# Writing the attention exponentials to PSUM and normalising from there, in a fused attention and feed-forward kernel on one core

## The chip, the core and the metric

The kernel runs on one core of one Trainium2 chip. The core has five engines that take their instructions in order and meet only at semaphores: TensorE (PE in the profile, its weight loads PEld), VectorE (DVE), ScalarE (ACT), GpSimd (POOL) and SyncE (SP, which issues DMAs here). TensorE writes its results to PSUM, a memory of 8 banks that VectorE and ScalarE can read and write; everything else lies in SBUF. The metric is the device time of the whole program in microseconds (us), the median of three runs.

## The reference

The program is a local attention (4 batches, 8 heads, 576 positions, head size 64, a window of the last 64 positions) followed by two feed-forward parts without a residual. Cut to what matters:

```python
scores = (q @ k.T) / sqrt(64)
scores = where(0 <= i - j < 64, scores, -1e9)
scores = scores - scores.max(-1)
attn   = exp(scores)
attn   = attn / (attn.sum(-1) + 1e-09)
x      = attn @ v                        # (2304, 512)
x      = ((x @ w1) * (x @ w2)) @ w3 @ w_out
h      = x @ w_in                        # (2304, 2048)
return (h * sigmoid(h)) @ w_out2
```

The weights arrive as float64 and are turned into float32, or into a high and a low part, on the chip.

## The kernel before

**Attention.** The 2304 tokens are cut into 18 units of 128, the 8 heads into 4 pairs, so there are 72 groups g, of one unit and one pair each. For a group, `scores(g)` multiplies queries with 192 keys for each of two heads into one PSUM tile `s` (128 x 2 x 192 float32, one bank, one buffer); two VectorE instructions on line 344 add the mask, scale and store the negated scores in the SBUF tile `sm` and their minimum in `nm`. `exps(g)` runs two ScalarE instructions (line 355, one for each head) that replace `sm` by its exponential in place and sum it into a small tile `es`. `normalise(g)` is three VectorE instructions: a sum of `es` (363), a reciprocal (365) and a product over `sm` in place (367). `transposes(g)` (377) has TensorE transpose `sm` in three pieces into the PSUM tile `t` (one bank, one buffer); `split_t(g)` copies it out on ScalarE (383, or 387 and 389) and, for later groups, takes the rounding remainder on VectorE (390, 392). `values(g)` multiplies with v into `o`.

**Two kinds of groups.** `plain(g)` is true for the first 17 groups (0 to 16), whose products run in float32. The other 55 use high and low parts.

**What sets the order.** The order on each engine is the order in which the code is written. `half(h)` does half a group: the even half of group g issues `scores(g)`, `values(g-2)`, `transposes(g-1)` with their copies, then `exps(g)`; the odd half issues `normalise(g)`, the sum of the values of g-2 (`total`: lines 419 and 420 on ScalarE, 421 and 422 on VectorE, 423 on GpSimd), and the preparation of the next queries and keys (297 on ScalarE, 309 on VectorE, 303 on GpSimd). `halves_to` puts one half before each unit of the dense work. In the first part (`phase_w`, up to about 91 us) that work is the conversion of the weights and the product of w3 and w_out (`accw`). In blocks 0 to 5 of 384 tokens (`phase_a`) a unit is 12 TensorE products of 128x384: first 16 units of x @ w1 and x @ w2 (`ab`, line 618; ScalarE copies one result, line 632, and VectorE multiplies the other into it, line 634, after which ScalarE casts it, line 85), then 8 units of the product with w3 @ w_out (`x`, line 648, copied out on line 601). `split_x` rounds the attention's result for the next block (lines 85 and 88, out of tile `xr`). The attention of the last group ends at about 403 us; what follows is the second feed-forward part, TensorE work without attention.

**Banks.** `s`, `t`, `o` and the conversion's `z` have one PSUM bank each, the accumulators of the dense work four.

Of the kernel before, what the change touches and what calls it, by code (L numbers as in the profile page):

```python
# [9 lines left out]
F32 = mybir.dt.float32  # L10
# [3 lines left out]
AF = mybir.ActivationFunctionType  # L14
ALU = mybir.AluOpType
# [19 lines left out]
def mask_kind(u):  # L35
    at = (u * 128) % S
    if at == 0:
        return 1
    return 2 if at + 128 > S else 0
# [3 lines left out]
def tile_window_attention_ffn(ctx, tc, qkv, qkp, vp, mask, w1, w2, w3t, w_out, w_in, w_out2, out):  # L43
# [7 lines left out]
    nc = tc.nc  # L51
# [5 lines left out]
    psa = late.enter_context(tc.tile_pool(name="psa", bufs=1, space=PSUM))  # L57
# [155 lines left out]
    def fill(n=1):  # L213

        for _ in range(min(n, len(parts))):
            parts.pop(0)()
# [18 lines left out]
    def drain():  # L235
# [7 lines left out]
    qk_raw, v_raw, qk_st, v_st, s_st, p_st = {}, {}, {}, {}, {}, {}  # L243
# [6 lines left out]
    sums_of = [  # L250
        att.tile([128, 16], F32, name=f"es{i}", tag=f"es{i}", bufs=1)[:, 0:4].rearrange("p (h n) -> p h n", h=2)
        for i in range(2)
    ]
# [7 lines left out]
    def plain(g):  # L261


        return g < PLAIN

    def place(g):
        blk, r = divmod(g, 3 * NPAIR)
        return blk * 3 + r % 3, r // 3
# [55 lines left out]
    def scores(g):  # L324
        s_ps = psa.tile([128, 2, 192], F32, name=f"s{g}", tag="s")
        t = qk_raw.pop(g) if plain(g) else qk_st.pop(g)
        if plain(g):
            k = t.rearrange("p (h n) -> p h n", h=2)[:, :, 0:192]
            nc.tensor.matmul(s_ps, lhsT=t[:, 192:320], rhs=k, start=True, stop=True)
        else:  # L330
            for h in range(2):

                nc.tensor.matmul(  # L333
                    s_ps[:, h], lhsT=t[:, 128 + h * 128 : 256 + h * 128],
                    rhs=t[:, 384 + h * 192 : 576 + h * 192], start=(h == 0), stop=False,
                )
            nc.tensor.matmul(s_ps, lhsT=t[:, 0:128], rhs=k_lo[g % 2], start=False, stop=True)
        nm = att.tile([128, 2], F32, name=f"nm{g}", tag="nm", bufs=2)
        rs = att.tile([128, 2], F32, name=f"rs{g}", tag="rs", bufs=2)
        fill(2)  # L340
        at = mask_at[mask_kind(place(g)[0])]
        for h in range(2):

            nc.vector.tensor_tensor_reduce(  # L344
                out=sm[g % 2][:, h, :], in0=s_ps[:, h, :], in1=consts[:, at + 64 - 64 * h : at + 256 - 64 * h],
                op0=ALU.add, op1=ALU.min, scale=-(D ** -0.5), scalar=3.0e38, accum_out=nm[:, h : h + 1],
            )
        fill()
        s_st[g] = (nm, rs)

    def exps(g):
        nm, rs = s_st[g]
        for h in range(2):
            x = sm[g % 2][:, h, :]
            nc.scalar.activation(  # L355
                out=x, in_=x, func=AF.Exp, scale=-1.0, bias=nm[:, h : h + 1], accum_out=sums_of[g % 2][:, h, 0:1]
            )

    def normalise(g):
        _, rs = s_st.pop(g)  # L360
        x = sm[g % 2]
        fill()
        nc.vector.tensor_reduce(out=rs, in_=sums_of[g % 2], axis=mybir.AxisListType.X, op=ALU.add)
        fill()
        nc.vector.reciprocal(out=rs, in_=rs)
        fill()
        nc.vector.tensor_tensor(out=x, in0=x, in1=rs.unsqueeze(2).to_broadcast([128, 2, 192]), op=ALU.mult)

    def transposes(g):

# [56 lines left out]
    def half(h):  # L427
# [4 lines left out]
        if not odd:  # L432
            if g < NG:
                scores(g)
# [7 lines left out]
            if g < NG:  # L442
                exps(g)
        else:
            if g < NG:
                normalise(g)
# [36 lines left out]
    def phase_w():  # L483
# [63 lines left out]
        for f in line[1].stage1():  # L547
            f()
        scores(0)
        spin(1)  # L550
        line[2].stage0(0)
        exps(0)
        line[2].stage0(1)
        for f in line[2].stage1():
# [118 lines left out]
    with tc.manual_schedule():  # L673
# [58 lines left out]
        for f in (0, 1, 2, 3, 4, 5, None, None, None, 6, 7, 8, 9, 10, 11, 12, 13, 14, 15):  # L732
# [3 lines left out]
            tag = f"w{f if f < 6 else f + 10 if f < 14 else f - 8}"  # L736
# [404 lines left out]
```

## Time and profile before

| | us |
|---|---|
| median of 3 runs | 841.74 (841.4 to 841.82) |
| the profiled execution, its own time | 841.24 |
| span of that execution in the profile | 839.5 |
| TensorE busy in it | 827.4 (99%) |
| VectorE / ScalarE / GpSimd busy | 615.3 / 561.2 / 529.7 |

The profiled execution's own time is 1.74 us above its span; these lie outside of what the profile shows. A timeline row gives the start in us from the span's beginning, the duration in us, the engine, the line of the kernel, the operation, its output and inputs by the program's names, their shapes and how many instructions the row merges; square brackets tell how long the engine sat idle before it and on what the idle time ended. A busy TensorE is not one at its peak, since a product's recorded time overlaps the next one's. The rows themselves stand below.

### The profile page before, as it was taken

The page shows a single profiled execution, that of the slowest core. Times are in us where ns is not written, and L with a number is a line of the kernel's source. Part 1 is how long each engine was busy: PE and PEld are TensorE (multiplying, and loading weights), DVE is VectorE, ACT ScalarE, POOL GpSimd, SP SyncE. Part 2 cuts the span into 40 slices and gives each one's busy share as a digit, 9 for nine tenths or more (in the row PEclk, how much of TensorE's full clock was granted, in tenths as well). Part 3 has the DMA queues.
Part 4 walks back from the last instruction along what each step waited for, and adds up shares of the span by engine and source line. Part 5 has one row for each costly group of instructions (what it writes and reads, how often), then busy time and mean ns, then how long its engine had stood idle before and what let it go on. Part 6 is the DMA issues. An engine that isn't in the chain of part 4 may idle for free.

```text
span 839.5 us, 14173 instructions
## 1 busy us (share of the span) xinstructions
PE 827.4 (99%) x4418; PEld 745.9 (89%) x4418; DVE 615.3 (73%) x1424; ACT 561.2 (67%) x1390; POOL 529.7 (63%) x588
## 2 busy tenths in 40 slices
PE   7999999999999999999999999999999999999998
PEld 3555799999999999999999988888888888988986
DVE  7889877688888888888368698998644567644544
ACT  6889778898898898898556566556543446443433
POOL 5768666677777677677565577876454456454441
PEclk9999999999999999999999999999999999999999
DMA  9998234444544544543433522301301201201002
GB/s 320 330 321 279 72 107 128 149 127 133 167 150 142 169 156 145 170 157 103 155 134 120 194 76 76 125 26 51 102 26 56 95 26 64 88 25 51 1 1 75
DMA packets 54682, 102.66 MB, mean 122 GB/s; under 512 B 5200, under 2 KB 32592, under 8 KB 54608
## 3 DMA queue, kind: packets, MB, share of 16 engines
q1 hardware_dynamic: 51008, 96.91, 35.5%
q10 hardware_dynamic: 3600, 4.85, 1.6%
q8 instruction: 35, 0.57, 0.3%
q14 instruction: 39, 0.32, 0.1%
HBM read 88.11 MB, written 13.63 MB: 121 GB/s over the span
## 4 chain that ended last, share of the span: by engine, by line
PE 69%; POOL 8%; ACT 6%; issue 4%; DVE 1%; ACTq 0%; POOLq 0%; DVEq 0%
PE o L882 24%; PE ab L618 14%; PE hy L828 12%; PE hx L828 9%; PE x L648 6%; POOL klo L303 2%; POOL vhl L321 1%; ACT sm L355 1%; PE t L377 1%; POOL xr L423 1%; ACT qkhi L297 1%; POOL p L88 1%; POOL cv_b L189 1%; PE o L411 1%; PE s L333 1%
## 5 line engine op out<-in xcount | busy, mean ns | idle before, releaser
L882 PE MATMUL o<-hl,gp 128*128 128x512 f32 x504 | 133.3, 394 | 0.0
L618 PE MATMUL ab<-xa,hl 128*128 128x384 f32 x576 | 119.0, 341 | 0.0
L828 PE MATMUL hy<-xop,j 128*128 128x384 f32 x576 | 115.9, 335 | 0.0
L618 PE MATMUL ab<-xb,hl 128*128 128x384 f32 x570 | 115.2, 334 | 0.0
L88 POOL TENSOR_TENSOR gp<-tmp,gp 128x384 fp32r<-128x384 f32 x56 | 64.1, 1145 | 77.5 <-ACT gp L85 75.9
L828 PEld LDWEIGHTS hy<-xop,j 128*128 128x128 f32 x576 | 102.6, 188 | 9.0 <-DVE tmp L722 1.0
L882 PEld LDWEIGHTS o<-hl,gp 128*128 128x128 f32 x504 | 93.1, 188 | 13.1
L618 PEld LDWEIGHTS ab<-xb,hl 128*128 128x128 f32 x570 | 100.3, 188 | 0.0
L618 PEld LDWEIGHTS ab<-xa,hl 128*128 128x128 f32 x576 | 99.1, 188 | 0.0
L844 ACT ACTIVATE tmp<-hx 128x384 f32<-128x384 f32 x48 | 23.6, 492 | 111.5 <-DVE hx L722 67.8
L722 DVE TENSOR_TENSOR tmp<-hy,tmp 128x384 f32<-128x384 f32 x96 | 53.2, 554 | 56.1 <-PE hy L828 51.5
L828 PE MATMUL hx<-xop,j 128*128 128x384 f32 x432 | 86.6, 335 | 0.0
L882 PE MATMUL o<-hl,gq 128*128 128x512 f32 x324 | 85.9, 393 | 0.0
L88 POOL TENSOR_TENSOR gq<-tmp,gq 128x384 fp32r<-128x384 f32 x36 | 39.0, 1084 | 74.3 <-ACT gq L85 74.3
L828 PEld LDWEIGHTS hx<-xop,j 128*128 128x128 f32 x432 | 76.8, 188 | 4.1
L423 POOL TENSOR_TENSOR xr<-ot 128x128 f32<-128x128 f32 x55 | 32.7, 594 | 73.7 <-DVE ot L422 65.5
L303 POOL TENSOR_TENSOR klo<-qk,qkhi 64x192 fp32r<-64x192 f32 x110 | 67.2, 611 | 7.6 <-ACT qkhi L297 2.7
L882 PEld LDWEIGHTS o<-hl,gq 128*128 128x128 f32 x324 | 60.3, 188 | 11.2
L648 PE MATMUL x<-p,wp 128*128 128x384 f32 x360 | 69.6, 339 | 0.0
L355 ACT ACTIVATE sm<-sm,nm 128x192 f32<-128x192 f32 x144 | 64.5, 450 | 3.9 <-DVE nm L344 2.5
L648 PEld LDWEIGHTS x<-p,wp 128*128 128x128 f32 x360 | 61.9, 188 | 0.0
L145 POOL TENSOR_TENSOR cv_b<-cv_b,cv_r 128x512 int32<-128x512 int32 x32 | 48.6, 1520 | 18.8 <-DVE cv_b L141 9.4
(146 smaller groups left out, 1896.7 us busy)
## 6 DMA issues: line engine op xcount, KB each, us to landing
qk<-in_qkv SPq DMA_DIRECT2D x55, 384.0 KB, 3.1
words<-in_w_out SPq DMA_DIRECT2D x24, 512.0 KB, 5.4
r<-w_in SPq DMA_DIRECT2D x22, 512.0 KB, 3.4
words<-in_w3t SPq DMA_DIRECT2D x16, 512.0 KB, 6.5
words<-in_w SPq DMA_DIRECT2D x16, 512.0 KB, 6.2
xe<-in_w_in SPq DMA_DIRECT2D x16, 512.0 KB, 4.8
v<-in_qkv SPq DMA_DIRECT2D x55, 96.0 KB, 2.7
x2d<-x2s ACTq DMA_DIRECT2D x24, 192.0 KB, 1.9
```

Of the source, the lines that this page charges most:

```text
L88: (nc.vector if eng_lo == "dve" else nc.gpsimd).tensor_tensor(out=lo, in0=src, in1=f32(hi), op=ALU.subtract)
L145: nc.gpsimd.tensor_tensor(out=x, in0=b, in1=self.r, op=ALU.add)
L189: nc.gpsimd.tensor_tensor(out=self.b, in0=self.b, in1=self.r, op=ALU.add)
L303: nc.gpsimd.tensor_tensor(out=k_lo[g % 2][hs, h * 192 : h * 192 + 192], in0=t[hs, n], in1=f32(hi[hs, n]), op=ALU.subtract)
L355: nc.scalar.activation(out=x, in_=x, func=AF.Exp, scale=-1.0, bias=nm[:, h : h + 1], accum_out=sums_of[g % 2][:, h, 0:1])
L423: nc.gpsimd.tensor_tensor(out=xr[:, c, r : r + 128], in0=t[:, 0:128], in1=t[:, 128:256], op=ALU.add)
L618: nc.tensor.matmul(acc, lhsT=w[:, l, fs], rhs=x[k // 2][:, k % 2, r, :], start=(k == 0 and n == 0), stop=(k == 3 and n == 2),)
L648: nc.tensor.matmul(acc, lhsT=wp[f][:, l, o * 128 : (o + 1) * 128], rhs=p[f][:, r, :], start=(f == 0 and n == 0), stop=(f == 7 and n == 2),)
L722: eng.tensor_tensor(out=out, in0=a, in1=b, op=op)
L828: nc.tensor.matmul(bank[name], lhsT=w[:, l, at + kt], rhs=x[:, kt, r, :], start=(fresh and kt == 0 and n == 0), stop=(kt == 1 and n == 2), ...
L844: nc.scalar.activation(out=sg, in_=src, func=AF.Sigmoid)
L882: nc.tensor.matmul(oacc[t], lhsT=g[:, l, cols], rhs=weights["out", 2 * p + i][:, r, :], start=(p == 0 and i == 0 and n == 0), stop=(p == P ...
```

## The change

The exponentials no longer replace `sm` in place. For the 17 plain groups `exps` takes a new tile `e` from the bank of the transposes' tile `t`; for the others it writes over the scores' own tile `s`, which the masked, scaled scores in `sm` have been read from. `normalise` multiplies out of that PSUM tile into `sm`, from which the transposes read as before.

```diff
-        s_st[g] = (nm, rs)
+        s_st[g] = [nm, rs, s_ps]
 
     def exps(g):
-        nm, rs = s_st[g]
+        nm = s_st[g][0]
+        if plain(g):
+            s_st[g][2] = psa.tile([128, 384], F32, name=f"e{g}", tag="t").rearrange("p (h n) -> p h n", h=2)
+        e = s_st[g][2]
         for h in range(2):
             x = sm[g % 2][:, h, :]
             nc.scalar.activation(
-                out=x, in_=x, func=AF.Exp, scale=-1.0, bias=nm[:, h : h + 1], accum_out=sums_of[g % 2][:, h, 0:1]
+                out=e[:, h, :], in_=x, func=AF.Exp, scale=-1.0, bias=nm[:, h : h + 1], accum_out=sums_of[g % 2][:, h, 0:1]
             )
 
     def normalise(g):
-        _, rs = s_st.pop(g)
+        _, rs, e = s_st.pop(g)
...
-        nc.vector.tensor_tensor(out=x, in0=x, in1=rs.unsqueeze(2).to_broadcast([128, 2, 192]), op=ALU.mult)
+        nc.vector.tensor_tensor(out=x, in0=e, in1=rs.unsqueeze(2).to_broadcast([128, 2, 192]), op=ALU.mult)
```

The instructions and their order stay the same on every engine. What changes beside operands is what they wait for. In the lists below a name in brackets is the semaphore of the engine that is waited for; three lines were added, so line 355 is 358 after the change, 377 is 380, 411 and 412 are 414 and 415.

On ScalarE, around the exponentials of group 56 (`nm56`), the program before has:

```order
L387 CAST pt3_957<-t55_4253 128x2x128 [waits PE_49,Activation_49]
L389 CAST pt1_955<-t55_4253 64x64 [waits Activation_49] x2
L355 ACTIVATE sm0_77,es0_86<-sm0_77,nm56_4244 128x192 [waits DVE_49,Activation_49] x2
L632 COPY a3_6_4278<-ab3_12_4265 128x384 [waits PE_49]
L419 COPY ot54_4283<-o54_4249 64x256 [waits Pool_49]
```

and the changed program:

```order
L390 CAST pt3_971<-t55_4270 128x2x128 [waits PE_49]
L392 CAST pt1_969<-t55_4270 64x64 x2
L358 ACTIVATE s56_4257,es0_86<-sm0_77,nm56_4261 128x192 [waits DVE_49,Activation_49]
L358 ACTIVATE s56_4257,es0_86<-sm0_77,nm56_4261 128x192 [waits Activation_49]
L635 COPY a3_6_4295<-ab3_12_4282 128x384 [waits PE_49]
L422 COPY ot54_4300<-o54_4266 64x256 [waits Pool_49]
```

Both write the same PSUM tile now. The count for which the second exponential waits on ScalarE's own semaphore is the one that the first raises when it is done; before, both waited for exponentials of two groups earlier. This holds for all 72 groups. In 16 of the plain groups the first exponential waits in the same way for the copy of line 383 right ahead of it, which reads the bank.

On TensorE, from the scores of group 57 to the transposes of group 56, the program before has:

```order
L333 MATMUL s57_4319<-qkhi57_4212 128x192 [waits DVE_49,PE_49,Activation_49]
L333 MATMUL s57_4319<-qkhi57_4212 128x192
L337 MATMUL s57_4319<-klo1_80,qkhi57_4212 128x384 [waits Pool_49]
L411 MATMUL o55_4329<-pt3_957,vhl55_4214 128x256 [waits DVE_49,Pool_49]
L411 MATMUL o55_4329<-pt3_957,vhl55_4214 128x256
L412 MATMUL o55_4329<-pt1_955,vhl55_4214 128x4x64 [waits DVE_49,Activation_49]
L377 MATMUL t56_4333<-consts_69,sm0_77 128x128 [waits DVE_49,PE_49,Activation_49]
```

and the changed program:

```order
L333 MATMUL s57_4336<-qkhi57_4229 128x192 [waits DVE_49,Activation_49]
L333 MATMUL s57_4336<-qkhi57_4229 128x192
L337 MATMUL s57_4336<-klo1_80,qkhi57_4229 128x384 [waits Pool_49]
L414 MATMUL o55_4346<-pt3_971,vhl55_4231 128x256 [waits Pool_49]
L414 MATMUL o55_4346<-pt3_971,vhl55_4231 128x256
L415 MATMUL o55_4346<-pt1_969,vhl55_4231 128x4x64
L380 MATMUL t56_4350<-consts_69,sm0_77 128x128 [waits PE_49]
```

VectorE's count on which the scores of 57 wait was that of line 344 of group 56; now it is that of the normalisation of group 56, for which the transposes of 56 waited before. The wait has moved from the seventh instruction of the row to the first. In the plain groups it stays with the transposes, since `e` does not lie in the scores' bank.

## Rows read from the trace of the kernel before

**Rows 1.** The page's part 1: busy us, share and instructions by engine.

```profile
PE 827.4 (99%) x4418; PEld 745.9 (89%) x4418; DVE 615.3 (73%) x1424; ACT 561.2 (67%) x1390; POOL 529.7 (63%) x588
```

**Rows 2.** Timeline of ScalarE: the exponentials of group 55.

```profile
313.98 0.46 ACT L355 ACTIVATE sm<-sm,nm 128x192 f32<-128x192 f32 x1
314.34 0.19 ACT L355 ACTIVATION_READ_ACCUMULATOR sm<-sm,nm 128x1 f32 x1
314.44 0.44 ACT L355 ACTIVATE sm<-sm,nm 128x192 f32<-128x192 f32 x1
```

**Rows 3.** Timeline of VectorE: normalising group 55 and what follows.

```profile
315.00 0.16 DVE L363 TENSOR_REDUCE rs<-es 128x2 f32<-128x4 f32 x1 [0.23 <-ACT sm L355]
315.20 0.17 DVE L365 RECIPROCAL rs<-rs 128x2 f32<-128x2 f32 x1
315.40 0.56 DVE L367 TENSOR_TENSOR sm<-sm,rs 128x384 f32<-128x384 f32 x1
...
316.34 0.42 DVE L421 TENSOR_TENSOR ot<-o,ot 64x256 f32<-64x256 f32 x1 [0.38 <-ACT ot L420]
...
317.58 0.56 DVE L634 TENSOR_TENSOR a<-ab,a 128x384 f32<-128x384 f32 x1
318.06 0.35 DVE L344 CUSTOM_DVE_ANT_0 sm<-s,consts 128x192 f32<-128x192 f32 x1
```

**Rows 4.** Timeline of ScalarE: the cast ahead of group 56's copies and exponentials.

```profile
318.17 0.52 ACT L85 CAST q<-a 128x384 fp32r<-128x384 f32 x1 [0.82 <-DVE a L634]
```

**Rows 5.** Timeline of VectorE: the sums (line 363) of groups 26 and 70.

```profile
160.28 0.16 DVE L363 TENSOR_REDUCE rs<-es 128x2 f32<-128x4 f32 x1 [0.22 <-ACT sm L355]
...
394.89 0.16 DVE L363 TENSOR_REDUCE rs<-es 128x2 f32<-128x4 f32 x1 [0.22 <-ACT sm L355]
```

**Rows 6.** Timeline of TensorE: scores of groups 29, 30 and 56, transposes of 55.

```profile
172.67 0.36 PE L333 MATMUL s<-qkhi 128*128 128x192 f32 x2
...
177.91 0.36 PE L333 MATMUL s<-qkhi 128*128 128x192 f32 x2
...
315.31 0.36 PE L333 MATMUL s<-qkhi 128*128 128x192 f32 x2
...
316.10 0.52 PE L377 MATMUL t<-consts,sm 128*128 128x128 f32 x3
```

**Rows 7.** Views of lines 367, 634, 844: count, shortest/median/longest ns, first and last start.

```profile
L367 DVE TENSOR_TENSOR sm<-sm,rs x72: 557/558/1642, 10.7 to 399.2; 128x384 f32<-128x384 f32 x72
...
L634 DVE TENSOR_TENSOR a<-ab,a x48: 546/558/561, 98.5 to 445.5; 128x384 f32<-128x384 f32 x48
...
L844 ACT ACTIVATE tmp<-hx x48: 482/492/494, 452.9 to 823.4; 128x384 f32<-128x384 f32 x48
L844 ACT ACTIVATE tmp<-tmp x48: 522/525/527, 463.6 to 828.3; 128x384 f32<-128x384 f32 x48
```

**Rows 8.** Waits, 140 to 166 us: waiter <- waited for: us in total, times, longest.

```profile
ACT pt L387 <- PE t L377: 2.0, 4, 0.7
```

**Rows 9.** Timeline around the change from block 2 to 3, group 49.

```profile
282.71 1.36 DVE L367 TENSOR_TENSOR sm<-sm,rs 128x384 f32<-128x384 f32 x1
...
285.65 0.52 ACT L85 CAST xb<-xr 128x384 fp32r<-128x384 f32 x1 [1.61 <-POOL xr L423]
```

**Rows 10.** Timeline of the start: groups 11 (77), 14 (93 to 95), 17 and 18 (114).

```profile
77.25 1.35 DVE L367 TENSOR_TENSOR sm<-sm,rs 128x384 f32<-128x384 f32 x1
...
93.12 0.43 ACT L383 COPY pw<-t 128x320 f32<-128x320 f32 x1
93.45 0.46 ACT L355 ACTIVATE sm<-sm,nm 128x192 f32<-128x192 f32 x1
...
95.02 1.56 DVE L367 TENSOR_TENSOR sm<-sm,rs 128x384 f32<-128x384 f32 x1
...
114.49 0.56 DVE L367 TENSOR_TENSOR sm<-sm,rs 128x384 f32<-128x384 f32 x1
...
114.67 0.36 PE L333 MATMUL s<-qkhi 128*128 128x192 f32 x2
```

## The prediction, made before the changed kernel was run

> **What bounds the kernel now.** I read the busy times first: TensorE is busy 99% of the span [rows 1], so the end moves only if TensorE waits longer or less. The change leaves its instructions and their order alone, so I looked for its waits: on the timeline, group by group, and from there at what releases them.
>
> After block 0, attention is a ring between ScalarE and VectorE. In group 55 the two exponentials start at 313.98 and 314.44 [rows 2]; behind them ScalarE has the copies of lines 632, 419 and 420, and these end the idle time of VectorE ahead of line 421 at 316.34, and VectorE's row goes on to line 634, which ends at 318.14 [rows 3]; this releases ScalarE's cast at 318.17 [rows 4], after which come the copies of the transposed tile and the exponentials of group 56. One turn is what passes between two line 363: from 160.28 (group 26) to 394.89 (group 70), 234.61 us for 44 turns, 5.33 each [rows 5]. TensorE needs less for a group: from 172.67 to 177.91, 5.24 [rows 6]. So TensorE starts ahead, its lead melts by 0.09 us a group, and in the later blocks it waits for normalised weights just before the transposes: normalising 55 ends at 315.96, the transposes start at 316.10 [rows 3, 6], 0.14 later. From then on the ring sets the pace, though TensorE looks full.
>
> The normalisation itself (line 367) is not on the ring: VectorE sits idle for 0.38 us behind it [rows 3].
>
> **The change part by part.** *1. Two exponentials in one PSUM tile.* The second one now waits until the first is done. Today it starts 0.455 us after it, while the first's accumulator is still being read: that read begins 0.36 after the first's start and ends at 0.55 [rows 2]. What a wait on the engine's own result costs is seen on VectorE, where line 365 waits for 363 in front of it: 315.00 + 0.16 to 315.20, some 0.035 us after its end [rows 3]. So the second exponential starts at 0.549 + 0.035 = 0.584 instead of 0.455: 0.129 us more for each group, on the ring, since line 632 and all behind it move along. No instruction of ScalarE before writes to PSUM, so its price has no row; the nearest is a function of the same engine that reads 384 columns from PSUM or from SBUF, 492 against 525 ns [rows 7]. As the read of the accumulator, not the write of the exponentials, is what the wait ends on, I take 0; if each exponential did get 0.033 shorter, the cost would be 0.129 - 0.066 = 0.063, and with a free wait as well 0.03. On the other side I allow 0.16.
>
> The Trainium skill speaks for less: "ScalarE: Activation LUTs", section "Step-by-step: what each stage is for", says that ScalarE writes to PSUM faster than to SBUF. No row here shows such a write; taken from the reads, the rule is the 0.063 above.
>
> From group 26 to group 70 there are 45 pairs of exponentials on the ring: 45 x 0.129 = **+5.8 us**. I count from there because just before, between 140 and 166 us, ScalarE's copies wait four times for the transposes [rows 8], so there the ring is in step with TensorE.
>
> *2. Normalising from PSUM.* Line 367 takes 0.56 us as a rule, but up to 1.64 [rows 7]: it reads two operands in SBUF, and the long ones run while GpSimd is at work on a SBUF pair of its own. Line 634, which takes one operand from PSUM, stays between 546 and 561 ns in all its 48 instances [rows 7]. So I expect 0.56 for all 72. In most groups that is worth nothing, since the instruction is either 0.56 already or off the ring. It counts where a long one is on the way to something late: at the three changes of block (into 2, 3 and 4; the pattern of group 49 also stands at 37 and 61) the normalisation of 1.36 us delays VectorE's part of the sum for `xr`, and ScalarE's cast at 285.65 waits 1.61 us for GpSimd's end of it [rows 9]. With 0.56 it comes 0.80 earlier, and the ring with it; what ends last there is still GpSimd's sum, so all 0.80 is won. 3 x 0.80 = **-2.4 us**. Should the cast turn out to be held by another thing, the gain is between 0 and that.
>
> *3. The scores wait for the normalisation.* The next scores overwrite the bank from which it reads. Between scores and transposes TensorE has 316.10 - 315.31 = 0.79 us of work [rows 6], which used to run before the wait and now runs behind it. Queued behind the waiting scores are the values, the transposes and the dense products; those who need them have room: the first reader of the scores (line 344) starts at 318.06, 2.7 us after them [rows 3, 6], and ScalarE's copies stand behind the cast of 318.17, 2.0 us after the transposes' start [rows 4, 6]. As the wait comes once per turn of 5.33 and TensorE needs 5.24 from one release to the next, it stays one fixed lag and does not add up: **+0.8 us**, once.
>
> *4. The start.* In group 17, the first whose exponentials lie in the scores' bank, the normalisation ends at 115.05, and the scores of 18 ran at 114.67 [rows 10]. With the 0.14 from above they could start at 115.19, +0.52. TensorE is full from there to block 1, so this stays. What reaches this point from before: the normalisation of group 14 takes 1.56 and holds up VectorE [rows 10]; at 0.56 it gives back 1.0. Against it stand four pairs of exponentials (14 to 17), 4 x 0.129, and the wait of the first exponential for the copy ahead of it: at 93.45 it starts before the copy's end at 93.55 [rows 10], so with 0.035 it loses 0.135, three times. Together 0.92, which eats the 1.0. Before 84 us the normalisation of group 11, 1.35 long, would give 0.8 [rows 10], while ScalarE, which is full there, loses up to 0.26 for each of four groups; I take 0, with -0.8 to +0.8 for the range. So **+0.5 us**.
>
> The waits that go (the transposes' on VectorE and ScalarE, those of the copies on ScalarE itself) were met when reached, and I give them nothing.
>
> *Sum:* 5.8 - 2.4 + 0.8 + 0.5 = +4.7 us. On the profiled execution, 841.24 us, that makes 845.9; the median of the runs shown lies 0.5 above it, so the forecast for the median is 841.74 + 4.7 = 846.4.
>
> **The rivals.**
>
> *A. The exponentials get cheaper in PSUM.* Then a pair costs 0.063 or less: 45 x 0.063 = 2.8, sum +1.7, 843.4; at 0.03 the sum is +0.3, 842.0. For it speaks the 33 ns of the reads; against it that the second waits for the read of the accumulator, which goes to SBUF as before.
>
> *B. Faster.* The freed normalisation is what counts: the pair costs nothing (the first exponential's accumulator is read that much earlier), and both long normalisations of the start reach TensorE, -0.8 and -0.9 in place of +0.5. Then 0 - 2.4 + 0.8 - 1.7 = -3.3, 838.4. This needs a pair below (3.3 - 1.7) / 45 = 0.036 us; the gap between line 363 and 365 alone is 0.035, so the overlap of 0.094 would have to survive a wait that forbids it.
>
> *C. The normalisation stays long.* If it still meets GpSimd with one operand in PSUM, the 2.4 go, and so does the 1.0 of group 14: +8.1, 849.8. Line 634's narrow spread speaks against it.
>
> *D. The moved wait is paid in each group.* If the ring ran through the scores, each of some 53 groups would lose up to 0.8 us: 884. Against it stand the 2.7 and 2.0 us of room in part 3.
>
> **How the numbers follow.** Forecast 0.66, A 0.18, B 0.09, C 0.05, D 0.02. The forecast's own range, from a pair of 0.10 to 0.15 us and the start's bounds, is 844.3 to 848.2. To leave out no more than 2 in 10 the range has to take in A and part of C and B: 840.8 to 848.8. A measurement of this kernel can tell about 0.2%, 1.7 us, from no change, that is 840.1 to 843.4. The forecast lies above that but for a small piece, A mostly within it, B below: faster 0.10, same 0.20, slower 0.70.
>
> **What would show it.** In the profile of the changed kernel: the second exponential some 0.58 us after the first instead of 0.455; sums of line 363 (366 then) 5.46 apart in the middle of blocks 1 to 4; the normalisation at 0.56 us throughout, and the cast of `xb` at the block changes waiting about 0.8 us instead of 1.6; TensorE waiting ahead of the scores of the later groups and no longer ahead of the transposes. It is wrong if the turns stay at 5.33, which would make it A or B by the pair's length; if TensorE's waits ahead of the scores come to more than a few us in all, it is D.

## The result and the profile after

| | median, us | runs | profiled execution: span | its time |
|---|---|---|---|---|
| before | 841.56 (841.18 to 841.82) | 5 | 839.5 | 841.24 |
| changed | 846.76 (846.27 to 847.57) | 5 | 845.0 | 846.76 |

The ratio is 1.0062, 95% interval 1.0051 to 1.0074. The change costs 5.2 us; 846.4 had been forecast, within 840.8 to 848.8. The end was met more closely than the way there: of the four terms one was right in size but is paid in part at three further places, one was right in size but partly eaten by that, one was too large and one too small.

The page's part 1 of the changed kernel, against [rows 1]: VectorE has 13 us less to do and ScalarE 8 us more on record, and TensorE, with the same instructions, falls from 99% to 98%.

```profile
PE 829.5 (98%) x4418; PEld 744.4 (88%) x4418; DVE 602.2 (71%) x1424; ACT 569.2 (67%) x1390; POOL 520.6 (62%) x588
```

The view of line 370 (367 before) by tile: count, shortest/median/longest ns, first and last start. Against the 557/558/1642 of [rows 7], not one normalisation is long any more.

```profile
L370 DVE TENSOR_TENSOR sm<-s,rs x55: 557/557/558, 116.3 to 404.3; 128x384 f32<-128x384 f32 x55
L370 DVE TENSOR_TENSOR sm<-e,rs x17: 557/557/558, 11.5 to 110.7; 128x384 f32<-128x384 f32 x17
```

Timeline of ScalarE, group 55 (start, duration, engine, line, operation), to be held against [rows 2]:

```profile
317.35 0.42 ACT L392 CAST pt<-t 64x64 fp32r<-64x64 f32 x2
317.68 0.42 ACT L358 ACTIVATE s<-sm,nm 128x192 f32<-128x192 f32 x1
318.11 0.20 ACT L358 ACTIVATION_READ_ACCUMULATOR s<-sm,nm 128x1 f32 x1
318.35 0.42 ACT L358 ACTIVATE s<-sm,nm 128x192 f32<-128x192 f32 x1
318.71 0.18 ACT L358 ACTIVATION_READ_ACCUMULATOR s<-sm,nm 128x1 f32 x1
318.92 0.48 ACT L635 COPY a<-ab 128x384 f32<-128x384 f32 x1
```

The second exponential starts 0.67 us after the first, not 0.455 as before nor 0.584 as forecast. But the first one starts earlier: 0.33 after the first copy of line 392, whose pair ends at 317.77, so it starts 0.09 ahead of their end. In the kernel before it stood 0.46 behind the start of these copies.

Timeline of VectorE and of TensorE for the same group, against [rows 3] and [rows 6]:

```profile
318.93 0.16 DVE L366 TENSOR_REDUCE rs<-es 128x2 f32<-128x4 f32 x1 [0.33 <-ACT s L358]
...
319.32 0.56 DVE L370 TENSOR_TENSOR sm<-s,rs 128x384 f32<-128x384 f32 x1
320.26 0.42 DVE L424 TENSOR_TENSOR ot<-o,ot 64x256 f32<-64x256 f32 x1 [0.38 <-ACT ot L423]
```

```profile
320.02 0.44 PE L333 MATMUL s<-qkhi 128*128 128x192 f32 x2
...
320.86 0.49 PE L380 MATMUL t<-consts,sm 128*128 128x128 f32 x3
```

The normalisation ends at 319.88; the scores of 56 start 0.14 later and the transposes 0.98 later. Before, it was the transposes that stood 0.14 behind it. This is the moved wait.

The sums of groups 26 and 70 [rows 5 before], on the timeline of VectorE:

```profile
162.76 0.16 DVE L366 TENSOR_REDUCE rs<-es 128x2 f32<-128x4 f32 x1 [0.33 <-ACT s L358]
...
399.61 0.16 DVE L366 TENSOR_REDUCE rs<-es 128x2 f32<-128x4 f32 x1 [0.33 <-ACT s L358]
```

They are 236.85 us apart, 2.24 more than before. Last, the change from block 2 to 3 on ScalarE: the cast waits 0.68 us for GpSimd's sum, where it waited 1.61 [rows 9].

```profile
289.11 0.51 ACT L85 CAST xb<-xr 128x384 fp32r<-128x384 f32 x1 [0.68 <-POOL xr L426]
```

**Where the time went.** I cut both executions at the same instructions: the transposes of groups 8 and 11, the scores of 18, the sums of 26, 34, 38, 46, 50, 58, 62 and 70, the transposes of 71. "Turns" are the 32 turns inside the blocks (26 to 34, 38 to 46, 50 to 58, 62 to 70), "changes" the 12 turns around the three block changes (34 to 38, 46 to 50, 58 to 62).

| us | to transposes 8 | to transposes 11 | to scores 18 | to sum 26 | turns | changes | sum 70 to transposes 71 | rest |
|---|---|---|---|---|---|---|---|---|
| before | 61.05 | 17.70 | 35.92 | 45.61 | 169.92 | 64.69 | 6.15 | 438.42 |
| changed | 61.88 | 18.06 | 37.07 | 45.75 | 172.34 | 64.51 | 6.95 | 438.42 |
| difference | +0.83 | +0.36 | +1.15 | +0.14 | +2.42 | -0.18 | +0.80 | 0.00 |

The differences add up to the 5.52 us between the two spans. The first, 0.83, mixes two things. TensorE and VectorE at groups 7 and 8, before:

```profile
55.02 0.50 PE L377 MATMUL t<-consts,sm 128*128 128x128 f32 x3
...
60.35 0.56 DVE L367 TENSOR_TENSOR sm<-sm,rs 128x384 f32<-128x384 f32 x1
...
61.05 0.52 PE L377 MATMUL t<-consts,sm 128*128 128x128 f32 x3 [0.79 <-ACT cv_r L128]
```

and in the changed kernel:

```profile
55.38 0.50 PE L380 MATMUL t<-consts,sm 128*128 128x128 f32 x3
...
61.18 0.56 DVE L370 TENSOR_TENSOR sm<-e,rs 128x384 f32<-128x384 f32 x1
...
61.88 0.52 PE L380 MATMUL t<-consts,sm 128*128 128x128 f32 x3 [0.99 <-ACT cv_r L128]
```

The transposes of 8 start 0.14 behind the end of their normalisation in both (60.91 and 61.74), so that is what they wait for; the releaser in brackets, a piece of the weights' conversion, is a wrong lead. From the transposes of 7 to those of 8 it is 6.03 before and 6.50 after by these rows. In all thirteen profiled executions this stretch repeats: 6.03 to 6.05 in the eight in which no exponential up to there waits for another or writes to PSUM, 6.32 and 6.33 in the two with the wait of the pair in SBUF, 6.51 (6.505 to 6.509) in the three with the early exponentials in PSUM. So 0.47 of the 0.83 belongs to the change. The other 0.36 lies ahead of the transposes of 4, where six executions whose instructions up to there are those of the kernel before lie some 2 us apart; they reach the transposes of 8 anywhere from 60.35 to 62.49. From the transposes of 4 to those of 7 all thirteen take 16.80 or 16.81.

The rest, +4.69, was the same to 0.05 us when the changed kernel was profiled again (below). The forecast's sum was +4.7. Behind the transposes of 7 the change costs 0.47 + 4.69 = 5.16, near the 5.2 of the medians. The table below begins at the transposes of 8, so this 0.47 is named where it counts.

### The profile page after: what moved, and what is told of

It is laid out like the page before. It is cut to its first block, busy times and chain, and to the rows that moved or that the text cites. A ratio compares the mean times of both kernels' runs of the same rounds, so it can differ in the third digit from the quotient of the medians.

```text
span 845.0 us, 13896 instructions
## 1 busy us (share of the span) xinstructions
PE 829.5 (98%) x4418; PEld 744.4 (88%) x4418; DVE 602.2 (71%) x1424; ACT 569.2 (67%) x1390; POOL 520.6 (62%) x588
## 4 chain that ended last, share of the span: by engine, by line
PE 81%; ACT 6%; DVE 2%; issue 2%; POOL 1%; DVEq 0%; POOLq 0%; ACTq 0%
PE o L885 24%; PE ab L621 18%; PE hy L831 12%; PE x L651 11%; PE hx L831 9%; PE t L380 2%; PE s L333 2%; PE o L414 1%; PE accw L585 1%; PE s L337 1%; ACT s L358 1%; ACT cv_b L125 1%; PE o L415 1%; ACT cv_r L128 1%; DVE a L637 1%
## 5 line engine op out<-in xcount | busy, mean ns | idle before, releaser
L85 ACT CAST gp<-tmp 128x384 fp32r<-128x384 f32 x56 | 28.8, 514 | 35.9 <-DVE tmp L725 35.1
```

The costliest lines, as they stand in the source:

```text
L85: nc.scalar.copy(out=hi, in_=src)
```

## The experiments

Each ratio compares 5 to 11 runs with runs of the kernel before, taken beside them. This table has the same cuts as the one above, without the rest behind the transposes of 71, which stays within 0.07 us; the text reads it.

| us | ratio (95%) | to tr. 8 | to tr. 11 | to scores 18 | to sum 26 | turns | changes | to tr. 71 |
|---|---|---|---|---|---|---|---|---|
| before | 1 | 61.05 | 17.70 | 35.92 | 45.61 | 169.92 | 64.69 | 6.15 |
| early groups only | 1.0013 (1.0004 to 1.0022) | 61.90 | 18.05 | 35.97 | 45.55 | 169.71 | 64.63 | 6.16 |
| later groups only | 1.0049 (1.0036 to 1.0061) | 61.89 | 17.69 | 36.57 | 45.75 | 172.36 | 64.48 | 6.95 |
| wait of the pair in SBUF | 1.0149 (1.0136 to 1.0163) | 61.79 | 17.84 | 36.03 | 46.08 | 180.96 | 65.12 | 6.16 |
| sums in the scores' bank | 1.0000 (0.9991 to 1.0009) | 60.35 | 17.70 | 36.44 | 45.57 | 169.80 | 63.59 | 6.96 |
| sums in the transposes' bank | 0.9974 (0.9964 to 0.9983) | 62.42 | 16.83 | 35.19 | 45.77 | 169.25 | 63.61 | 6.72 |
| the same, three groups | 0.9974 (0.9963 to 0.9984) | 62.49 | 17.72 | 35.89 | 45.61 | 169.77 | 62.25 | 6.47 |
| first exponential to PSUM | 0.9982 (0.9973 to 0.9991) | 61.13 | 17.70 | 35.87 | 45.50 | 168.30 | 64.50 | 6.15 |
| pair's wait and short normalisation | 1.0043 (1.0030 to 1.0055) | 61.92 | 17.91 | 35.61 | 46.26 | 172.88 | 64.22 | 6.18 |
| early groups and three | 0.9958 (0.9945 to 0.9970) | 61.80 | 16.82 | 35.13 | 45.61 | 169.46 | 62.61 | 6.46 |
| four groups | 0.9966 (0.9954 to 0.9979) | 61.62 | 16.91 | 35.92 | 45.61 | 169.79 | 62.30 | 6.46 |
| changed, again | 1.0065 (1.0051 to 1.0078) | 61.90 | 18.07 | 37.05 | 45.80 | 172.34 | 64.52 | 6.95 |

**One half at a time: the early groups.** The edit is to the changed kernel; the later groups go back to SBUF, in place.

```
-        if plain(g):
+        if not (plain(g)):
+            s_st[g][2] = sm[g % 2]
+        elif plain(g):
```

> The exponentials lie in the transposes' bank for the 17 float32 groups alone; all later groups work in SBUF as before. In the trace of the changed kernel TensorE is 0.39 us late at the transposes of group 11 and 1.54 late at the scores of group 18, of which the wait for the normalisation of 17 is the last piece. Theory: the early groups alone make 0.4 to 0.6 us of this, because without the wait of the scores of 18 the late normalisation of 17 still has some 0.5 us of room before its transposes: +0.5 us in all. Rival: what ScalarE loses in the early groups (0.9 us by group 17) sets the ring of the later ones: +1.0 us or more. Turns of the ring stay at 5.33.

Measured: ratio 1.0013 (0.3 to 1.9 us), about +1.1 us, which by itself would be the rival's number. The trace puts it elsewhere: 0.85 of the 0.95 in the span stand ahead of the transposes of group 8, 0.47 of them between the transposes of 7 and 8. Behind that point the early groups cost 0.35 at the transposes of 11 and 0.05 up to the scores of 18, as the theory had it; from there on the differences sum to -0.30, so the rival, by which the delay goes on into the ring, falls. Behind the transposes of 7 that leaves 0.47 + 0.10 = 0.57, the theory's +0.5. VectorE and TensorE around group 17:

```profile
116.15 0.56 DVE L372 TENSOR_TENSOR sm<-sm,rs 128x384 f32<-128x384 f32 x1
```

```profile
115.92 0.36 PE L333 MATMUL s<-qkhi 128*128 128x192 f32 x2
```

The scores of 18 run ahead of the normalisation of 17, which ends at 116.71. It stands 0.48 us further behind the scores of 14 than before (0.64 in the changed kernel), but no scores wait for it there.

**The later groups.**

```
-        if plain(g):
+        if not (not plain(g)):
+            s_st[g][2] = sm[g % 2]
+        elif plain(g):
```

The edit is again to the changed kernel; the branch behind `elif`, with the tile in the transposes' bank, is then never taken.

> The exponentials lie in the scores' bank for group 17 and all later ones; the 17 float32 groups work in SBUF as before. Theory: the ring's turns are 5.42 to 5.43 instead of 5.33, the scores of 18 wait 0.5 to 0.6 us, TensorE's lag at the transposes grows to 0.87 behind the normalisation: 0.6 + 2.2 + 0.8 = +3.6 us. Rival: the two halves of the change simply add up, so that with +0.5 for the early groups this one has +4.7.

Measured: ratio 1.0049, +4.2 by the medians (3.0 to 5.1 by the ratio, which holds the theory's number and the rival's); behind the transposes of 8 the differences sum to +3.8, near the theory's 3.6 and with its parts: 0.65 up to the scores of 18, turns of 5.42 to 5.43, 0.80 at the end. The rival isn't met: the two halves make 0.05 and 0.65 of the stretch before the scores of 18, the whole makes 1.15. The missing 0.45 arises only together: the late normalisation of 17 costs little while the scores need not wait for it, and all of it once they do. In the whole change it is these two rows, of VectorE and TensorE:

```profile
116.30 0.56 DVE L370 TENSOR_TENSOR sm<-s,rs 128x384 f32<-128x384 f32 x1
```

```profile
117.01 0.44 PE L333 MATMUL s<-qkhi 128*128 128x192 f32 x2 [0.92 <-ACT qkhi L297]
```

The normalisation ends at 116.86 and the scores start 0.15 behind it. The releaser in brackets is a wrong lead: VectorE's part of that cast's group starts only at 117.06, so the cast belongs to group 19. The 0.15 behind the normalisation is there in all three kernels in which these scores wait for it (this, the later groups alone, and the sums in the scores' bank below).

**The pair's wait alone, in SBUF.**

```
-        nc.vector.memset(t, 1.0e-9)
+        nc.vector.memset(t, 0.5)
...
-                out=x, in_=x, func=AF.Exp, scale=-1.0, bias=nm[:, h : h + 1], accum_out=sums_of[g % 2][:, h, 0:1]
+                out=x, in_=x, func=AF.Exp, scale=-1.0, bias=nm[:, h : h + 1], accum_out=sums_of[g % 2][:, 0, 0:1]
```

> Everything in SBUF as before, but both exponentials of a group add up into the same word, so that the second has to wait for the first; the other word stays at its start value, so the sums leave out the second head's part. No bank is shared and no wait of TensorE is new. Theory: the wait alone is the price of a turn, and the write to PSUM costs nothing: turns of 5.42 to 5.43 as in the changed kernel, 45 of them make +4.2, with the early groups +4.5 to +5. Rival 1: the wait costs 0.129 a turn as forecast and the write to PSUM gave some of it back: turns of 5.46, +6. Rival 2: the first exponential, which in the changed kernel starts 0.32 us after the copies of line 389 begin instead of 0.46, does so only where it writes to PSUM: then it stands at 0.46 here, otherwise at 0.32.

Measured: +12.6 us, which no theory had. Two things are in it. ScalarE first:

```profile
322.00 0.42 ACT L389 CAST pt<-t 64x64 fp32r<-64x64 f32 x2
322.45 0.46 ACT L355 ACTIVATE sm<-sm,nm 128x192 f32<-128x192 f32 x1
322.82 0.19 ACT L355 ACTIVATION_READ_ACCUMULATOR sm<-sm,nm 128x1 f32 x1
323.04 0.46 ACT L355 ACTIVATE sm<-sm,nm 128x192 f32<-128x192 f32 x1
323.40 0.19 ACT L355 ACTIVATION_READ_ACCUMULATOR sm<-sm,nm 128x1 f32 x1
```

The second exponential starts 0.58 after the first, which is the forecast's 0.584, and the plain turns are 5.47: rival 1 for the price of the wait. The first stands 0.45 behind the copies, not 0.33: rival 2, the early start comes with the write to PSUM. The other thing is new. Every third turn is 6.15, and the view of line 367 and VectorE and GpSimd around one of them show why:

```profile
L367 DVE TENSOR_TENSOR sm<-sm,rs x72: 557/559/1632, 10.8 to 412.2; 128x384 f32<-128x384 f32 x72
```

```profile
317.85 1.62 DVE L367 TENSOR_TENSOR sm<-sm,rs 128x384 f32<-128x384 f32 x1
```

```profile
316.80 1.02 POOL L88 TENSOR_TENSOR p<-a,p 128x384 fp32r<-128x384 f32 x1
317.78 1.28 POOL L189 TENSOR_TENSOR cv_b<-cv_b,cv_r 128x512 int32<-128x512 int32 x1
```

The later ring lets the normalisation fall on GpSimd's line 189, which has just begun; it takes 1.62, and line 421 behind it comes 0.7 late. Eleven of the 32 turns inside the blocks have such a one, 11 x 0.69 = 7.6 of the 11.0 us that the turns gained. So with the normalisation left long the wait of the pair costs 12.2 us behind the transposes of 8, and with a short one 3.1 (below). What the change's own, smaller delay of the pair would have met without the short normalisation no run shows.

**The moved wait without the pair's.** The two sums go into free columns of the scores' bank, so line 367 has one operand in PSUM and the next scores wait for it.

```
-        s_ps = psa.tile([128, 2, 192], F32, name=f"s{g}", tag="s")
+        s_all = psa.tile([128, 512], F32, name=f"s{g}", tag="s")
+        s_ps = s_all[:, 0:384].rearrange("p (h n) -> p h n", h=2)
...
-        rs = att.tile([128, 2], F32, name=f"rs{g}", tag="rs", bufs=2)
+        rs = att.tile([128, 2], F32, name=f"rs{g}", tag="rs", bufs=2) if plain(g) else s_all[:, 384:386]
```

> Exponentials in SBUF as before; for group 17 and later the two reciprocal sums lie in free columns of the scores' bank, so that the normalisation takes one operand from PSUM and the next scores wait for it, as in the change, but the second exponential doesn't wait for the first. Theory: the moved wait costs one lag of 0.8 us at the end and 0.5 at the scores of 18, and something at the block changes, where the short normalisations give up to 0.8 each back: turns 5.33, all normalisations from group 17 on 0.56, sum between -1 and +1. Rival: the moved wait is what makes the turns longer (5.42) or takes the gain of the block changes and more: +2 or above.

Measured: no difference, 0.9991 to 1.0009, as the theory summed it. Its parts: +0.52 to the scores of 18, +0.81 at the end, turns unchanged at 5.33 to 5.34, and -1.10 at the three changes, 0.37 each. A pair of columns as PSUM operand is enough to keep the instruction short:

```profile
L368 DVE TENSOR_TENSOR sm<-sm,s x55: 553/554/556, 113.8 to 398.1; 128x384 f32<-128x384 f32 x55
L368 DVE TENSOR_TENSOR sm<-sm,rs x17: 557/558/1554, 10.8 to 108.3; 128x384 f32<-128x384 f32 x17
```

**The short normalisation without any new wait.** The sums lie in the transposes' bank, for which the transposes have to wait anyway.

```
-        rs = att.tile([128, 2], F32, name=f"rs{g}", tag="rs", bufs=2)
+        rs = None if True else att.tile([128, 2], F32, name=f"rs{g}", tag="rs", bufs=2)
...
+        if rs is None:
+            t_of[g] = psa.tile([128, 512], F32, name=f"t{g}", tag="t")
+            rs = t_of[g][:, 384:386]
...
-        t_ps = psa.tile([128, 384], F32, name=f"t{g}", tag="t")
+        t_ps = t_of.pop(g) if g in t_of else psa.tile([128, 512], F32, name=f"t{g}", tag="t")
```

It was run for all groups, then for groups 37, 49 and 61 alone (`rs = None if g in (37, 49, 61) else att.tile(...)`).

> Exponentials in SBUF as before; the two reciprocal sums of every group lie in free columns of the transposes' bank, which the transposes have to wait for anyway. All 72 normalisations take one operand from PSUM; no score waits for a normalisation and no exponential for the other. Theory: the short normalisation gives 0.80 us at each of the three block changes, as forecast, and only the moved wait took part of it away (in the run with the sums in the scores' bank a change gave 0.37): from group 34 to 38 the sums are 20.8 us apart instead of 21.55; with 0.8 at the transposes of group 11 that makes -3.2 us. Rival: a change gives 0.37 here too, because something else ends last: 21.2 us, -1.9 in all.

> The same, but only for groups 37, 49 and 61, the last long normalisation at each block change. Theory: the long ones of the two groups ahead are off the path, so each change gives the same as with all of them short, 0.8 us, -2.4 in all. Rival: those of 35 and 36 hold up the ring too, and a change gives 0.4 or less: -1.2 or less.

Measured: 0.9974 both times, -2.2 us. For the three groups the theory holds: from 46 to 50 the sums are 20.73 apart instead of 21.57, so 0.84, and 0.81 over the three; the long ones of the two groups ahead are off the path. VectorE's two sums and ScalarE's cast:

```profile
267.70 0.16 DVE L366 TENSOR_REDUCE rs<-es 128x2 f32<-128x4 f32 x1 [0.23 <-ACT sm L355]
...
288.43 0.16 DVE L366 TENSOR_REDUCE rs<-es 128x2 f32<-128x4 f32 x1 [0.23 <-ACT sm L355]
```

```profile
285.33 0.52 ACT L85 CAST xb<-xr 128x384 fp32r<-128x384 f32 x1 [0.71 <-POOL xr L426]
```

With all groups the early part comes out (16.83 instead of 17.70 to the transposes of 11, 35.19 instead of 35.92 to the scores of 18), but the changes give 1.08 together, not 2.4; there the rival's number came. So did its reason: what ends last is TensorE, which no longer waits, and its turns are 0.03 us longer than with three groups, 5.274 against 5.244. Its scores of groups 21 and 33:

```profile
130.51 0.36 PE L333 MATMUL s<-qkhi 128*128 128x192 f32 x2
...
193.79 0.36 PE L333 MATMUL s<-qkhi 128*128 128x192 f32 x2
```

These twelve turns take TensorE 63.28, against 62.94 in the kernel before and with three groups. The sums of 38 and 50, twelve turns with a block change among them, lie 63.29 apart here, so the ring goes at TensorE's pace; they lie 63.90 apart before and 63.01 with three groups. In the run with the sums in the scores' bank, where a change gave nearly the same 0.37, the reason is another: its sums lie 63.43 apart, while its TensorE needs 62.92. From the scores of 18 to the transposes of 71 the run with all groups takes 285.35 us against 284.10 with three. The 0.03 stands for the most part in the products right behind the transposes, and again in the run with the pair's wait and the short normalisation below, the only other one with all 72 sums in this bank. No wait of TensorE shows there, and I can't say why its products lie further apart.

**The write to PSUM alone.**

```
-        s_st[g] = (nm, rs)
+        s_st[g] = (nm, rs, s_ps)
...
-        nm, rs = s_st[g]
+        nm, rs, e = s_st[g]
...
-                out=x, in_=x, func=AF.Exp, scale=-1.0, bias=nm[:, h : h + 1], accum_out=sums_of[g % 2][:, h, 0:1]
+                out=x if h or plain(g) else e[:, 0, :], in_=x, func=AF.Exp, scale=-1.0, bias=nm[:, h : h + 1], accum_out=sums_of[g % 2][:, h, 0:1]
```

> Everything as before, but from group 17 on the first exponential's result is written into the scores' bank, where nobody reads it; the normalisation takes the first head's weights as they were ahead of the exponential, so that head's exponentials are left out. Priced by itself is the write to PSUM, with no wait between the two exponentials. Theory: the first exponential, coming behind copies that write to SBUF, starts 0.1 us ahead of their end and its accumulator is read 0.037 us earlier; turns of 5.29 to 5.30 instead of 5.33, -1 us. Rival: the write to PSUM gains nothing without the wait: 5.33, no difference.

Measured: 0.9982, -1.4 us; the turns are 5.28. ScalarE:

```profile
317.63 0.42 ACT L389 CAST pt<-t 64x64 fp32r<-64x64 f32 x2
317.95 0.42 ACT L355 ACTIVATE s<-sm,nm 128x192 f32<-128x192 f32 x1
318.39 0.20 ACT L355 ACTIVATION_READ_ACCUMULATOR s<-sm,nm 128x1 f32 x1
318.50 0.44 ACT L355 ACTIVATE sm<-sm,nm 128x192 f32<-128x192 f32 x1
```

Again the first starts 0.32 behind the copies' start. Its accumulator is in at 318.59, 0.96 behind that start, where it took 1.00 in the run with the wait in SBUF: the theory's 0.04. So the write to PSUM is worth some 0.04 us a turn; the other 0.01 lies between the two copies of line 389, which stand closer since, as in the changed kernel, they don't wait for copies of two groups earlier any more.

**The pair's wait with the short normalisation.** The two edits above together.

> The forced wait of the second exponential in SBUF (both add up into one word, the other word keeps its start value, so the second head's sum is left out of it), and the reciprocal sums of all groups in the transposes' bank as in the run above. Theory: the wait in SBUF alone made turns of 5.47, and the rest of its 12.6 us came from normalisations that fell on GpSimd's work and took 1.6 us; with one operand in PSUM none is above 0.6 and the turns are 5.47 throughout: +3 to +4 us. Rival: the long normalisations were a consequence and the turns of 6.16 stay: +8 or more.

Measured: 1.0043, +3.6 by the ratio, +3.1 behind the transposes of 8. Every normalisation takes 553 to 556 ns, no turn of 6.15 is left, and the plain ones are 5.46: the theory. From 38 to 46 the sums are 43.22 apart, 0.89 more than before, seven turns of 0.13:

```profile
226.34 0.17 DVE L366 TENSOR_REDUCE t<-es 128x2 f32<-128x4 f32 x1 [0.37 <-ACT sm L355]
...
269.56 0.17 DVE L366 TENSOR_REDUCE t<-es 128x2 f32<-128x4 f32 x1 [0.37 <-ACT sm L355]
```

**The gains together.** The sums in the transposes' bank for the 17 early groups and 37, 49, 61; then for 11, 37, 49, 61; and the changed kernel beside them.

> Exponentials in SBUF as before; the reciprocal sums in the transposes' bank for the 17 float32 groups and for groups 37, 49 and 61 alone. Theory: the two gains stand in different places and add up: 1.6 us less from the transposes of group 8 to the scores of 18, as with all groups, and 0.8 less at each block change, as with the three: -3.6 to -4.0 us, the fastest so far. Rival: TensorE, which then stands nearly full from group 18 on, keeps the early gain from reaching the end, or takes that of the block changes: -2.2.

> The same for groups 11, 37, 49 and 61 alone. Theory: of the long normalisations of the early groups that of 11 gives 0.8 us at its transposes and those of 14 to 16 the other 0.7 by the scores of 18: -3.0 us here. Rival: the one of 11 is all that counts early: the same as with all 17, -3.6 or more.

> The changed kernel itself, to have it on the same chip as the two others: 5 us above the kernel before; the stretch from the transposes of group 8 to the scores of 18 is 55.1 us instead of 53.6, whatever time the start takes ahead of it.

Measured: 838.09 us, ratio 0.9958, faster than both kernels; 838.66, 0.9966; and 846.92, 1.0065. The first has 1.67 less up to the scores of 18 and 2.23 less from there to the transposes of 71, so the two gains add up. The second takes 3.00 less in all behind the transposes of 8, as its theory had it. In it group 11 alone gives 0.79 at its transposes, which was the 0.8 of the forecast's part 4; the other early groups give as much again ahead of the scores of 18 (35.13 against 35.92). The changed kernel takes 55.12 from the transposes of 8 to the scores of 18, where 55.1 was expected.

## Why the prediction was right, step by step

**What bounds.** Right. Within the blocks the ring of ScalarE and VectorE sets the pace: a turn takes 5.33 before, 5.42 to 5.43 in the changed kernel, and every experiment that touched only ScalarE's pair moved it (5.28, 5.46).

**Part 1, the pair.** The wait itself was priced right: 0.129 from [rows 2, 3], 0.13 a turn in SBUF. The write to PSUM was taken at nothing, and that was wrong: by itself it gives back 0.04 to 0.05, and in the changed kernel the turn has grown by 0.09, which is 0.13 less that. The 0.066 for two exponentials, which the forecast had from reads of PSUM and SBUF and kept as a bound, was nearer; the choice of zero rested on the read of the accumulator being the end, and that read starts earlier too, because the first exponential starts before the copies ahead of it are done. The second, behind its wait, gains nothing: from its start to the end of its read 0.54 here and 0.55 in SBUF. The Trainium skill ("ScalarE: Activation LUTs", "Step-by-step: what each stage is for") says that ScalarE writes faster to PSUM than to SBUF. These traces agree in sign; the rule's weight here is this 0.04, for the first of two. The forecast's estimate by that rule, 0.063 for a pair, lies 0.03 below the measured 0.09, and the one without it 0.04 above. The count was too high as well: inside the blocks 32 turns grew by 2.42, where 32 x 0.129 made 4.1. The first turn of each block didn't grow (4.97 before, 4.98 after), the others by 0.09 at most.

**Part 2, the normalisation.** Right in all it said of itself: 0.56 throughout, the cast's wait down from 1.61 to 0.68, and 0.81 us a change where nothing else was altered. That "all 0.80 is won" fell, by part 3. One more row bears out the cause: a PSUM operand of two columns is enough. The Trainium skill has the rule that an instruction of VectorE with two inputs in SBUF contends with a read of GpSimd's, and one with a single such input doesn't ("SBUF — State Buffer", "Who interferes with whom"). The 1.62 us against 553 to 558 ns agree.

**Part 3, the moved wait.** The lag at the end is 0.80, as forecast, and the turns don't pay it, so rival D is out. But the claim that it is paid once failed: at each block change it is paid again in part. With the sums in the scores' bank a change gains 0.37, with no moved wait 0.81. In the changed kernel its four turns grow by 4 x 0.093, and as it still comes out 0.06 shorter, it gains 0.43. The turn from 34 to 35 shows it. In the kernel before, its transposes start at 204.70 and ScalarE's copy doesn't wait for them:

```profile
205.28 0.37 ACT L387 CAST pt<-t 128x256 fp32r<-128x256 f32 x1
```

TensorE and ScalarE of the changed kernel:

```profile
207.36 0.44 PE L333 MATMUL s<-qkhi 128*128 128x192 f32 x2 [0.42 <-DVE sm L370]
...
208.18 0.49 PE L380 MATMUL t<-consts,sm 128*128 128x128 f32 x3
```

```profile
208.71 0.37 ACT L390 CAST pt<-t 128x256 fp32r<-128x256 f32 x1 [0.31 <-PE t L380]
```

In the middle of a block ScalarE comes 2.0 us after the transposes; here no cast that waits for line 637 stands ahead of the copies, ScalarE comes first and waits 0.31 for the transposes. The room was read from the middle of a block [rows 3, 4, 6] and taken for all turns.

**Part 4, the start.** Forecast +0.5, measured +1.98 from the transposes of 7 to the scores of 18. The wait of those scores was right: 0.52 with the sums in the scores' bank. For the stretch before 84 us I took 0 with 0.8 on both sides, and 0.83 came, just outside: 0.47 at the transposes of 8 and 0.36 up to those of 11. The gain of group 11 was right (0.8), but two things outweigh it. A piece of the weights' conversion ahead of it on VectorE, line 157, waits for ScalarE and starts 4.21 behind the transposes of 10 (at 71.96) instead of 3.59 (at 71.13), and then takes 1.64 instead of 1.10, with GpSimd at work on lines 157 and 145 beside it. Before, and in the changed kernel:

```profile
74.72 1.10 DVE L157 TENSOR_TENSOR hl<-cv_b,hl 128x512 fp32r<-128x512 f32 x1 [0.38 <-ACT hl L153]
```

```profile
76.17 1.64 DVE L157 TENSOR_TENSOR hl<-cv_b,hl 128x512 fp32r<-128x512 f32 x1 [0.68 <-ACT hl L153]
```

The 0.62 and the 0.47 make 1.09, near the 4 x 0.26 = 1.04 that the forecast allowed ScalarE at most; the 0.54 of a stretched neighbour it didn't have, and 1.09 + 0.54 - 0.79 = 0.84. That is one step that failed. The other, behind that stretch, is the 1.0 us that the normalisation of 14 was to "give back". Shortened alone, it brings the exponentials of 15 forward by 0.36, and those of 17 by no more: VectorE then waits 0.5 us for ScalarE ahead of line 637. In the run with the two gains:

```profile
94.66 0.55 DVE L370 TENSOR_TENSOR sm<-sm,t 128x384 f32<-128x384 f32 x1
...
97.74 0.56 DVE L637 TENSOR_TENSOR a<-ab,a 128x384 f32<-128x384 f32 x1 [0.50 <-ACT a L629]
```

The loss on ScalarE was near the forecast: the exponentials of 17 come 0.50 later behind the scores of 14, with the 0.36 gained a loss of 0.86, where 0.92 less the pair of 17 made 0.79. So 0.64 is missing from the term, and 0.52 + 0.64 is the 1.16 by which the scores of 18 stand later behind those of 14.

**The sum.** Forecast 0.5 + (5.8 - 2.4) + 0.8 = 4.7; measured 1.98 + 0.14 + (2.42 - 0.18) + 0.80 = 5.16. The start was 1.5 to 1.6 too low and the ring 1.2 too high. That the total fits to half a microsecond is luck, since these two errors nearly cancel; the sign is not: the ring and the lag alone make 3.0.

**Rivals.** A had the right mechanism and too much of it, and its time of 842.0 to 843.4 lacked the start. B needed a pair below 0.036; it cost 0.09. C is excluded by the view of line 370. D holds at three places, for about half of its 0.8, and nowhere else.

## What to carry to other kernels

A wait for an engine's own result was priced here from a pair of another engine that waits so already (0.035 us on VectorE, and 0.03 on ScalarE from the read's end at 323.01 to 323.04), but the same edit in another memory shifts the start of the instruction, and that shift decided here between 5.46 and 5.42 us a turn. Room behind a moved wait has to be read in every kind of turn, at the seams too, and a gain upstream counts only up to the next thing that is late. If one short operand in PSUM removes a contention, put that operand into a bank for which the consumer waits anyway: the reciprocal sums of twenty groups in the transposes' bank brought 3.6 us with none of the costs of moving the exponentials. Two traces are best compared from a point behind which they repeat: cut at the transposes of 4 or 7 instead of 8, 0.47 us that looked like noise belongs to the change.

## What the runs showed that was not expected

- One instruction that starts later can be stretched by another engine's: with the pair's wait in SBUF, 0.13 us a turn became 0.35 on average ((180.96 - 169.92) / 32), since eleven of 32 normalisations then met a GpSimd instruction and took 1.6 us. In the changed kernel's start the short normalisation of 11 is outweighed in part by a piece of the conversion ahead of it that takes 1.64 instead of 1.10 us.
- ScalarE starts an exponential that writes to PSUM 0.09 us before the copies ahead of it, which write to SBUF, are done; the same exponential writing to SBUF starts 0.025 after their end.
- The same instructions at the program's start reach the same point up to 2 us apart in different executions (60.35 to 62.49), all of it ahead of the transposes of group 4; the stretch from there to the transposes of 7 took 16.80 or 16.81 in all thirteen.
- With the sums of all 72 groups in the transposes' bank, TensorE's turns are 0.03 us longer than with those of twenty (scores 5.27 against 5.24 apart), at a granted clock of 0.999 and 1.0 over the run; the cause stays open.
